# Softmax maxima in a fused attention and gated-MLP kernel: GpSimd keeps the maximum over partitions, VectorE takes the rest

## The chip, the cores and the metric

The kernel runs on one core of a Trainium2 chip. The metric is the device time of one execution in microseconds, as the median of several runs. A core has TensorE (PE, matrix products), VectorE (DVE), ScalarE (ACT), GpSimd (POOL) and SyncE (SP), which here only starts transfers. Each works through its own instructions in order. The work of an instruction starts when the semaphores it waits for have been raised, and whatever stands behind a waiting instruction on the same engine waits with it.

## The reference

```python
g = sigmoid((x * gate_w).sum(-1, keepdims=True))     # x: [1, 2048, 448]
q, k, v = split_heads(x @ wqkv)                      # 16 heads of 28
scores = einsum("bhqd,bhkd->bhqk", q, k) * 28 ** -0.5
a = (softmax(scores) @ v) @ wo
gate = x @ W_gate                                    # 448 -> 1792
h = (gate * (gate > 0)) * (x @ W_up)
b = h @ W_down                                       # 1792 -> 448
out = g * a + (1 - g) * b
```

Everything is float32. The products of the projections and of the MLP are made from a high and a low part of each operand, eleven matmuls ("passes") for one product of 448 terms.

## The kernel before

There are three stretches. The first projects q, k and v and writes q and k to DRAM. The second is the attention, with part of the MLP's gate and up products mixed in. The third holds what is left of these, the output projection and the down projection.

The attention is done in 32 rounds. Round v does one visit: head v // 2 and one half of its 16 key tiles of 128, against all 2048 queries in 4 blocks of 512 (`TB`). A visit has 16 score pairs. One pair is two matmuls into one score buffer of two PSUM banks (`score`, L250 to L267); there are three such buffers, taken in turn by `ps_w`, and the row maxima use the same three.

For 12 of the 16 pairs (query blocks 0 to 2) the maximum of each query over all keys is known ahead. It comes from "row maxima" (`smax`, L161 to L176): the scores are made a second time with queries on partitions, two matmuls into a score buffer, and VectorE reduces them (L171). The maxima of a head are turned round and written into extra rows of Q (`smax_end`), so that the matmul subtracts them itself, and ScalarE applies exp straight from PSUM (L262). Each round has 12 row maxima except the last three, which have none.

The other 4 pairs (query block 3) take another way:

- ScalarE copies the pair from PSUM into a P tile in SBUF (L264).
- `block_max` (L211 to L232) takes a running maximum over the key tiles on VectorE, elementwise into the tile `rm` (L224, L225, L227, L230). In a head's second visit it starts from the maximum of the first.
- `all_max` (L236) has GpSimd take the maximum over the 128 partitions.
- `take_max` (L241) subtracts it from the P tile, four key tiles at once (128 x 2048); two of these make the four pairs.
- `take_exp` (L248) has ScalarE apply exp in place.

`pv` (L593 to L611) then multiplies P by V, in two parts of 32 matmuls each; the second visit's result is added to the first's. `rescale` (L574 to L589) scales the first visit's result for query block 3 by exp of the difference of the two maxima: a subtraction (L585), an exp (L588), a product (L589), once in every second round.

The MLP's units are passes (`gu_mm`, L547) followed by a ReLU on ScalarE (L557) and a product on VectorE (L560); the result h is sent to DRAM (`spill_h`, L566). Weights are split on ScalarE and GpSimd in the first rounds (`split_f`) and reloaded by SP later (`load_f`, L539).

The order of everything in a round is written out by hand, one mark per step, as strings: FIRST for round 0, LONG for most, WIDE for four rounds with 44 passes instead of 33, LATE for the last three. The marks:

```text
s  a score pair (with its copy or exp)     m  a row maximum
x  one pass of the MLP                     n  a head's row maxima turned round
A  all_max                                 d, g  take_max on VectorE, on GpSimd
e  take_exp                                c, f  rescale, first and second step
w  split the weights of the next round     P, Q  the two parts of PV
```

`AHEAD` says how many of the next visit's pairs are already scored at the end of a round; these are always pairs of query block 3.

Of the kernel before, what the change touches and what calls it, by code (L numbers as in the profile page):

```python
# [13 lines left out]
OP = mybir.AluOpType  # L14
# [5 lines left out]
P = 128  # L20
# [9 lines left out]
TB = 512  # L30
NK = S // P
# [6 lines left out]

EARLY = (5, 4, 4, 3, 2, 2, 1, 1)

AHEAD = 2

NP = 10

FIRST = "xxxmxAsmxlsumxxxsmxxsmxsmxsmsmxsgxmdsexxxmexxmsxxmwxPQ"

LONG = "mmnsxxxsxxxsxxssmxxsxxsxxAmsxxxsmsxxgmxsxmxsxsxcmsxexxmxgmsxfxsexxxmmPwQ"

WIDE = "msxsxxsxxxsxmnxAxxxsmxxxxssxxxmxxxsxxssxxmxsxxmmxsxgexxmxxgmxxxCsxxsxmxxsmxeFsxmwPQ"

LATE = "ssnxxsxxxxxxsxsxxxxxssxxxxxxxsxssxxAdxxsxxxxdsxsxexCxsxxxsxxexfxwsxxxPQ"

ROUNDS = [(FIRST, 2)] + [(WIDE, 4) if k % 7 == 2 else (LONG, 3) for k in range(2 * H - 4)] + [(LATE, 4)] * 3

# [12 lines left out]
def gated_mix_kernel(ctx, tc, x, wq, wo, wgu, wd, out):  # L67
    nc = tc.nc
# [23 lines left out]
    def ps_w(name):  # L92
        if turns[0] is not None:
            turns[0] += 1
            if turns[0] % 3 == 0:
                return third[0].tile([P, 2, TB], F32, tag="w", bufs=1, name=name)
        return psum.tile([P, 2, TB], F32, tag="mx", bufs=2, name=name)

    def ps_x(name):
        return psum.tile([P, TB], F32, tag="x", bufs=2, name=name)  # L100
# [23 lines left out]
    h_d = {}  # L124
# [8 lines left out]
    def last_q(name, dt=F32R):  # L133
        return vp.tile([P, 4, TB], dt, name=name, tag="Q2", bufs=1)

    def p_slot(k, name, dt=F32):
        if k in (5, 6):
            return V[:, k - 3].rearrange("p k h d -> p (k h d)").rearrange("p (j t) -> p j t", t=TB)
        return (vp if k < 5 else att).tile([P, 4, TB], dt, name=name, tag=f"P{k}", bufs=1)
# [50 lines left out]
    AT, QUAD, slots = {}, {}, iter(range(10 ** 6))  # L190
# [17 lines left out]
    todo_max, todo_sub, todo_exp, todo_all = [], [], [], []  # L208
    RM = {}

    def block_max(v, j, k, q):  # L211

        n = TQ[v // 2]
        b = j - NB + n
        if (v, b) not in RM:
            if b == 0:
                rm = att.tile([P, max(TQ), TB], F32, name=f"rm_{v}", tag=f"rm{v % 2}", bufs=1)
                for c in range(n):
                    RM[v, c] = rm[:, c]
        r, p = RM[v, b], QUAD[q]  # L220
        c = k % 4
        if k % (NK // 2) == 0:
            if v % 2:
                nc.vector.tensor_tensor(r, p[:, c], RM[v - 1, b], op=OP.max)  # L224
                nc.vector.tensor_tensor(r, p[:, c + 1], r, op=OP.max)  # L225
            else:
                nc.vector.tensor_tensor(r, p[:, c], p[:, c + 1], op=OP.max)  # L227
        else:
            for d in range(2):
                nc.vector.tensor_tensor(r, p[:, c + d], r, op=OP.max)  # L230
        if k % (NK // 2) == NK // 2 - 2:
            todo_all.append((v, b, [(v, j, i) for i in (k // 4 - 1, k // 4)]))  # L232

# [2 lines left out]
        nc.gpsimd.partition_all_reduce(RM[v, b], RM[v, b], P, bass_isa.ReduceOp.max)  # L236
        todo_sub.extend((v, b, q) for q in quads)

    def take_max(engine):
        v, b, q = todo_sub.pop(0)  # L240
        engine.tensor_tensor(QUAD[q], QUAD[q], RM[v, b].unsqueeze(1).to_broadcast([P, 4, TB]), op=OP.subtract)  # L241
        todo_exp.append(q)

    def take_exp():
# [5 lines left out]
    def score(late=True):  # L250

        v, done, q, half, chunks = stream.pop(0)
        h = v // 2
        if q not in QUAD:
            QUAD[q] = p_slot(next(slots) % NP, f"P_{v}_{q[1]}_{q[2]}")
        ps = ps_w(f"s_{v}_{chunks[0][0]}_{chunks[0][1]}")
        for c, (k, j) in enumerate(chunks):
            nc.tensor.matmul(ps[:, c], K[h % 3][:, k * P:(k + 1) * P], Q[h][:, j * TB:(j + 1) * TB], start=True, stop=True)  # L258
            AT[v, k, j] = QUAD[q][:, 2 * half + c]
        dst = QUAD[q][:, 2 * half:2 * half + 2]  # L260
        if done:
            nc.scalar.activation(dst, ps, AF.Exp, scale=SCALE)  # L262
        else:
            nc.scalar.activation(dst, ps, AF.Copy)  # L264
            todo_max.append((v, chunks[0][1], chunks[0][0], q))
        while late and todo_max:
            block_max(*todo_max.pop(0))  # L267

    X = {}

# [17 lines left out]
    with tc.tile_pool(name="qkv", bufs=1) as pa:  # L288
# [135 lines left out]
        ps = ps_x("warm_ps")  # L424
# [130 lines left out]
    def relu(i, ps):  # L555
        RL[i] = fe.tile([P, TB], F32, name=f"rl_{i}", tag="rl", bufs=2)
        nc.scalar.activation(RL[i], ps, AF.Relu)  # L557

    def hidden(i, ps, h):
        nc.vector.tensor_tensor(h, ps, RL.pop(i), op=OP.mult)  # L560

    def spill_h(i, ps):
        h = fe.tile([P, TB], F32, name=f"h_{i}", tag="h", bufs=2)
        hidden(i, ps, h)
        h_d[i] = dram.tile([P, TB], F32, name=f"h_d_{i}")
        nc.gpsimd.dma_start(h_d[i], h)  # L566


    NI = H * NK
    OS, LS = {}, {}  # L570

    RS = {}

    def rescale(v, part, engine):  # L574

        h = v // 2
        n = TQ[h]
        if v % 2 == 0 or n == 0:
            return
        rows = slice(32 * (NB - n), P)  # L580
        if part == 0:
            RS[h] = fe.tile([P, TB], F32, name=f"rs_{h}", tag="rb", bufs=1)
            for b in range(n):
                r = slice(32 * (NB - n + b), 32 * (NB - n + b) + 32)
                engine.tensor_tensor(RS[h][r], RM[v - 1, b][r], RM[v, b][r], op=OP.subtract)  # L585
        else:
            d = RS.pop(h)[rows]
            nc.scalar.activation(d, d, AF.Exp, scale=SCALE)  # L588
            engine.tensor_tensor(OS[h][rows], OS[h][rows], d, op=OP.mult)  # L589

    PO = {}

# [69 lines left out]
    for v, (order, nu) in enumerate(ROUNDS):  # L662
        todo = list(range(nxt, nxt + nu))
        nxt += nu
        small_things(2 * v)
        passes = [(*divmod(k, 2), n) for k in todo for n in range(NT)]
        units = []
        ns = 0
        for o in order:
            if o == "x" and not passes:  # L670
                continue
            if o == "s":
                ns += 1
                if ns == 8:
                    small_things(2 * v + 1)
                if stream:
                    score()
            elif o == "m":
                if m < len(maxima):
                    smax(m)  # L680
                    m += 1
            elif o == "x":
                i, half, n = passes.pop(0)
                if n == 0:
                    units.append((i, half, ps_x(f"gu_{i}_{half}")))
                gu_mm(units[-1][2], i, half, n)
                if n == NT - 1:
                    i, half, ps = units.pop()
                    spill_h(i, ps) if half else relu(i, ps)
                    if half:  # L690
                        load_f(i + 2)
            elif o == "n":
                if v % 2 and v < 2 * H - 1:
                    smax_end(v // 2 + 1)
            elif o == "w":
                ready = nxt + (ROUNDS[v + 1][1] if v + 1 < len(ROUNDS) else 2)
                ready = min(ready + ready % 2, 2 * NF)
                while parts < ready:
                    split_f(parts // 2, act_high, pool_low, (parts % 2,))
                    parts += 1  # L700
                    if parts % 2 == 0:
                        fetch_f(parts // 2 + 1)
            elif o == "A":
                all_max()
            elif o == "d":
                take_max(nc.vector)
            elif o == "g":
                take_max(nc.gpsimd)
            elif o == "e":
                take_exp()  # L710
            elif o in "cCfF":
                rescale(v, "cf".index(o.lower()), nc.gpsimd if o in "cf" else nc.vector)
            elif o == "l":
                sends.pop()()
            elif o == "u":
                split_f(0, act_high, pool_low, (1,))
                QS.append(last_q("Q2"))
                nc.gpsimd.memset(f32(QS[2])[96:128], 0.0)
                load_k(2)
                load_q(2)  # L720
                fetch_f(2)
                parts = 2
            elif o in "PQ":
                pv(v, "PQ".index(o))
        left = [k for k in todo_exp + todo_sub + todo_all if k[0] == v]
        assert not passes and not left and v not in PO or len(stream) == max(0, 16 * (2 * H - 1 - v) - AHEAD), (v, passes, left, len(stream) + 16 * (v + 1))
    assert not stream and m == len(maxima), (len(stream), m)
# [183 lines left out]
```

## Time and profile before

| | us |
|---|---|
| median of 3 runs | 1543.4 (1539.19 to 1546.63) |
| the profiled execution | 1536.65 |
| its span, first to last instruction | 1534.9 |

| engine | busy us | share of the span |
|---|---|---|
| TensorE, matmul | 1296.2 | 84% |
| VectorE | 899.7 | 59% |
| ScalarE | 772.5 | 50% |
| GpSimd | 523.1 | 34% |

The mean clock granted to TensorE is 0.926 of full speed. Rounds end with the copy or addition of the PV result: round 0 at 181.42 us of the span, round 28 at 1234.55, round 31 at 1326.91. "Busy" of TensorE is modelled and contains the overlap of matmuls in its pipeline, so that 84% doesn't mean that only 16% can be won.

In the rows of the profile, `a <- b` names what an instruction writes and reads, `xN` is a count, and a bracket at the end of a timeline row tells how long the engine stood idle before it and what released it.

### The profile page before, as it was taken

The page shows a single profiled execution, that of the slowest core. Times are in us where ns is not written, and L with a number is a line of the kernel's source. Part 1 is how long each engine was busy: PE and PEld are TensorE (multiplying, and loading weights), DVE is VectorE, ACT ScalarE, POOL GpSimd, SP SyncE. Part 2 cuts the span into 40 slices and gives each one's busy share as a digit, 9 for nine tenths or more (in the row PEclk, how much of TensorE's full clock was granted, in tenths as well). Part 3 has the DMA queues.
Part 4 walks back from the last instruction along what each step waited for, and adds up shares of the span by engine and source line. Part 5 has one row for each costly group of instructions (what it writes and reads, how often), then busy time and mean ns, then how long its engine had stood idle before and what let it go on. Part 6 is the DMA issues. An engine that isn't in the chain of part 4 may idle for free. (4 is left out here: it accounts for less than half of the span.)

```text
span 1534.9 us, 17075 instructions
## 1 busy us (share of the span) xinstructions
PE 1296.2 (84%) x6431; PEld 880.0 (57%) x6431; DVE 899.7 (59%) x939; ACT 772.5 (50%) x894; POOL 523.1 (34%) x327
## 2 busy tenths in 40 slices
PE   9997897887877789797978978778879788999998
PEld 6885554554544456464645545445545444689998
DVE  6465675565656557575755756666657533355333
ACT  5224675665555456475645655555646555522221
POOL 4221444435352333333333342524334211253110
PEclk9999898998989899898989989899999889999999
DMA  9663642333324232231425232313251122573442
GB/s 315 227 244 123 189 96 102 107 95 97 100 79 136 96 106 74 82 98 58 137 71 140 75 89 90 94 62 94 69 164 47 63 68 82 182 229 115 134 141 80
DMA packets 60687, 178.38 MB, mean 116 GB/s; under 512 B 13730, under 2 KB 20578, under 8 KB 55970
## 3 DMA queue, kind: packets, MB, share of 16 engines
q1 hardware_dynamic: 49388, 136.32, 30.5%
q0 software_dynamic: 10784, 40.51, 7.0%
q8 instruction: 51, 0.84, 0.2%
q10 hardware_dynamic: 432, 0.46, 0.1%
q14 instruction: 32, 0.26, 0.1%
HBM read 118.58 MB, written 58.87 MB: 116 GB/s over the span
## 5 line engine op out<-in xcount | busy, mean ns | idle before, releaser
L171 DVE TENSOR_REDUCE mx<-sm 128x1 f32<-128x1024 f32 x384 | 461.7, 1221 | 177.2 <-PE sm L169 176.9
L169 PE MATMUL sm<-K,Q 128*128 128x512 f32 x768 | 254.3, 419 | 172.9 <-ACT P L264 122.0
L547 PE MATMUL gu<-X,wg 128*128 128x512 f32 x1232 | 381.3, 400 | 17.4 <-POOL wg L112 11.6
L258 PE MATMUL s<-Q,K 128*128 128x512 f32 x1024 | 321.1, 401 | 25.2 <-ACT P L262 21.5
L262 ACT ACTIVATE P<-s 128x1024 f32<-128x1024 f32 x306 | 299.3, 1026 | 44.6 <-PE s L258 40.2
L169 PEld LDWEIGHTS sm<-K,Q 128*128 128x128 f32 x768 | 139.9, 196 | 244.1 <-ACT P L264 129.9
L601 PE MATMUL po<-P,V 128*32 128x512 f32 x1640 | 265.6, 671 | 15.8 <-ACT rl L557 13.4
L547 PEld LDWEIGHTS gu<-X,wg 128*128 128x128 f32 x1232 | 233.7, 190 | 76.1 <-POOL wg L112 12.0
L241 POOL TENSOR_TENSOR P<-P,rm 128x2048 f32<-128x2048 f32 x45 | 204.0, 4537 | 159.9 <-issue 144.6
L258 PEld LDWEIGHTS s<-Q,K 128*128 128x128 f32 x1024 | 184.6, 190 | 87.6 <-ACT P L262 28.9
L248 ACT ACTIVATE P<-P 128x2048 f32<-128x2048 f32 x52 | 99.4, 1911 | 203.0 <-POOL P L241 182.0
L601 PEld LDWEIGHTS po<-P,V 128*32 128x32 f32 x1640 | 66.8, 122 | 165.3 <-issue 141.9
L264 ACT ACTIVATE P<-s 128x1024 f32<-128x1024 f32 x104 | 104.5, 1019 | 75.3 <-PE s L258 73.0
L566 POOL DMA_DIRECT2D h_d<-h x56 | 38.3, 683 | 304.7 <-DVE h L560 288.5
L810 PE MATMUL acc<-WD,hh 128*128 128x448 f32 x672 | 138.5, 365 | 0.0
L601 PE MATMUL po<-V 128*32 128x512 f32 x408 | 136.1, 673 | 0.6 <-ACT V L248 0.6
L236 POOL PARTITION_ALL_REDUCE rm<-rm x32 | 57.6, 1801 | 230.1 <-DVE rm L230 81.7
L810 PEld LDWEIGHTS acc<-WD,hh 128*128 128x128 f32 x672 | 126.2, 188 | 10.4
L230 DVE TENSOR_TENSOR rm<-P,rm 128x512 f32<-128x512 f32 x156 | 118.1, 757 | 22.2 <-ACT P L264 14.8
L103 ACT ACTIVATE hh<-hr 128x512 fp32r<-128x512 f32 x56 | 35.3, 632 | 119.0 <-PE acc L810 116.5
L262 ACT ACTIVATE V<-s 128x1024 f32<-128x1024 f32 x78 | 77.2, 1026 | 24.7 <-PE s L258 24.0
L227 DVE TENSOR_TENSOR rm<-P 128x512 f32<-128x512 f32 x13 | 37.5, 2888 | 88.0 <-ACT P L264 87.1
(86 smaller groups left out, 1026.6 us busy)
## 6 DMA issues: line engine op xcount, KB each, us to landing
wg<-ws_d SPq DMA_DIRECT2D x42, 896.0 KB
K<-qk_d SPq DMA_DIRECT2D x64, 224.0 KB
Q<-qk_d SPq DMA_DIRECT2D x64, 224.0 KB
h_d<-h POOLq DMA_DIRECT2D x56, 256.0 KB, 2.5
hr<-h_d SPq DMA_DIRECT2D x56, 256.0 KB
ws_d<-wg SPq DMA_DIRECT2D x14, 896.0 KB
qk_d<-st POOLq DMA_DIRECT2D x21, 512.0 KB, 3.2
wgr<-wgu SPq DMA_DIRECT2D x13, 512.0 KB
```

The lines of the kernel that those rows point to most:

```text
L169: nc.tensor.matmul(ps[:, c, :], Q[h][:, u * P:(u + 1) * P], K[h % 3][:, k0:k0 + TB], start=True, stop=True)
L171: nc.vector.tensor_reduce(MX[h][:, 2 * u + half:2 * u + half + 1], ps, axis=AX.XY, op=OP.max)
L230: nc.vector.tensor_tensor(r, p[:, c + d], r, op=OP.max)
L236: nc.gpsimd.partition_all_reduce(RM[v, b], RM[v, b], P, bass_isa.ReduceOp.max)
L241: engine.tensor_tensor(QUAD[q], QUAD[q], RM[v, b].unsqueeze(1).to_broadcast([P, 4, TB]), op=OP.subtract)
L248: nc.scalar.activation(q, q, AF.Exp, scale=SCALE)
L258: nc.tensor.matmul(ps[:, c], K[h % 3][:, k * P:(k + 1) * P], Q[h][:, j * TB:(j + 1) * TB], start=True, stop=True)
L262: nc.scalar.activation(dst, ps, AF.Exp, scale=SCALE)
L264: nc.scalar.activation(dst, ps, AF.Copy)
L547: nc.tensor.matmul(ps, WS[i][:, s, a], xf(i // NF, b), start=(n == 0), stop=(n == NT - 1))
L601: nc.tensor.matmul(po[32 * j:32 * j + 32], V[:, h // 4 % 2, k, h % 4], AT.pop((v, k, j)), start=(k == k0), stop=(k == k0 + NK // 2 - 1))
L810: nc.tensor.matmul(ACC[i // NF][t][:, :D], HH[i][:, a, t * P:(t + 1) * P], WD[:, f, b], start=(f == 0 and n == 0), stop=(f == NF - 1 and n ...
```

## The change

- `block_max` reads the scores from PSUM instead of from ScalarE's copy in SBUF (only the pairs scored before round 0 still use the copy). The first maximum of a head takes one tile from PSUM and the other from the copy, as VectorE takes one operand from PSUM here.
- `take_max` is always on VectorE; before, 57 of its 64 instructions were GpSimd's (`g`).
- `rescale`'s subtraction and product are always on VectorE; before, they were GpSimd's in LONG and partly in LATE.
- The transfer of h to DRAM is started by SP instead of GpSimd.
- Three pairs of the next visit are scored ahead instead of two.
- All four order strings are new. In LONG, A moves from the 26th mark to the 5th, and the two `take_max` to the 35th and 60th.

```diff
-AHEAD = 2
+AHEAD = 3
-FIRST = "xxxmxAsmxlsumxxxsmxxsmxsmxsmsmxsgxmdsexxxmexxmsxxmwxPQ"
-LONG = "mmnsxxxsxxxsxxssmxxsxxsxxAmsxxxsmsxxgmxsxmxsxsxcmsxexxmxgmsxfxsexxxmmPwQ"
-WIDE = "msxsxxsxxxsxmnxAxxxsmxxxxssxxxmxxxsxxssxxmxsxxmmxsxgexxmxxgmxxxCsxxsxmxxsmxeFsxmwPQ"
-LATE = "ssnxxsxxxxxxsxsxxxxxssxxxxxxxsxssxxAdxxsxxxxdsxsxexCxsxxxsxxexfxwsxxxPQ"
+FIRST = "AmxmxsmxmxxlxsxumsmmmxxxsxdxxxsxssmxxmxsmmxdexxsxsewsPQ"
+LONG = "ssmnAxxxxsmxsxmxsmxxxmsmxxxsmxxmxsdxsxxxsxsmxxxsmxxmexxsmxxdxxcsxsefwsPQ"
+WIDE = "smnmxxxxxxxsxxmxxxxmsxmxxsmxxsAmxsxmxxsxsmxdxsxxsssxxxmxxxcsxmsxxdxxmxxxxexsxewsPfQ"
+LATE = "snwsxxAxdxxxsxxsxxxsxxdsxxxxcsxxsxxxsxxxsxxxxsxsxxxxsxxxxxexxxsxxessPfQ"
...
-        r, p = RM[v, b], QUAD[q]
-        c = k % 4
-        if k % (NK // 2) == 0:
-            if v % 2:
-                nc.vector.tensor_tensor(r, p[:, c], RM[v - 1, b], op=OP.max)
-                nc.vector.tensor_tensor(r, p[:, c + 1], r, op=OP.max)
-            else:
-                nc.vector.tensor_tensor(r, p[:, c], p[:, c + 1], op=OP.max)
+        r = RM[v, b]
+        if k % (NK // 2):
+            parts = [(p[:, c], r) for c in range(2)]
+        elif v % 2:
+            parts = [(p[:, 0], RM[v - 1, b]), (p[:, 1], r)]
         else:
-            for d in range(2):
-                nc.vector.tensor_tensor(r, p[:, c + d], r, op=OP.max)
+            parts = [(p[:, 0], q[:, 1])]
+        for x, y in parts:
+            nc.vector.tensor_tensor(r, x, y, op=OP.max)
...
-    def take_max(engine):
+    def take_max():
         v, b, q = todo_sub.pop(0)
-        engine.tensor_tensor(QUAD[q], QUAD[q], RM[v, b].unsqueeze(1).to_broadcast([P, 4, TB]), op=OP.subtract)
+        nc.vector.tensor_tensor(QUAD[q], QUAD[q], RM[v, b].unsqueeze(1).to_broadcast([P, 4, TB]), op=OP.subtract)
...
             nc.scalar.activation(dst, ps, AF.Copy)
-            todo_max.append((v, chunks[0][1], chunks[0][0], q))
-        while late and todo_max:
-            block_max(*todo_max.pop(0))
+            job = (v, chunks[0][1], chunks[0][0], ps if late else dst, dst)
+            if late:
+                block_max(*job)
+            else:
+                todo_max.append(job)
...
-        nc.gpsimd.dma_start(h_d[i], h)
+        nc.sync.dma_start(h_d[i], h)
...
-                engine.tensor_tensor(RS[h][r], RM[v - 1, b][r], RM[v, b][r], op=OP.subtract)
+                nc.vector.tensor_tensor(RS[h][r], RM[v - 1, b][r], RM[v, b][r], op=OP.subtract)
...
-            engine.tensor_tensor(OS[h][rows], OS[h][rows], d, op=OP.mult)
+            nc.vector.tensor_tensor(OS[h][rows], OS[h][rows], d, op=OP.mult)
```

More of the change, by code (lines that the diff above doesn't have):

```diff
@@ L209, in gated_mix_kernel, with block_max @@
     RM = {}
-    def block_max(v, j, k, q):
+    def block_max(v, j, k, p, q):
         n = TQ[v // 2]
@@ L572, in gated_mix_kernel, with rescale @@
     RS = {}
-    def rescale(v, part, engine):
+    def rescale(v, part):
         h = v // 2
@@ L705, in gated_mix_kernel @@
             elif o == "d":
-                take_max(nc.vector)
-            elif o == "g":
-                take_max(nc.gpsimd)
+                take_max()
             elif o == "e":
                 take_exp()
-            elif o in "cCfF":
-                rescale(v, "cf".index(o.lower()), nc.gpsimd if o in "cf" else nc.vector)
+            elif o in "cf":
+                rescale(v, "cf".index(o))
             elif o == "l":
```

## The prediction, made before the changed kernel was run

> **What bounds the kernel now.** I read the page first, then the waits, then the timeline of one pair of rounds.
>
> ```profile
> span 1534.9 us, 17075 instructions
> PE 1296.2 (84%) x6431; PEld 880.0 (57%) x6431; DVE 899.7 (59%) x939; ACT 772.5 (50%) x894; POOL 523.1 (34%) x327
> ...
> ACT P L248 <- POOL P L241: 182.0, 37, 11.5
> ...
> PE sm L169 <- ACT P L264: 122.0, 18, 11.0
> ...
> PE sm L169 <- ACT V L264: 41.5, 6, 11.1
> ...
> PE s L258 <- ACT P L262: 21.5, 4, 7.3
> ...
> PE po L601 <- ACT rl L557: 13.4, 3, 6.9
> ...
> PE gu L547 <- POOL wg L112: 11.6, 1, 11.6
> ```
>
> No engine is full, TensorE (PE) is the busiest, and it idles in few, long waits: 122.0 + 41.5 us in 24 waits for the ScalarE copy on L264. ScalarE itself waits 182.0 us for GpSimd's subtraction (L241). The timeline of one round shows the chain:
>
> ```profile
> 684.54 0.59 POOL L566 DMA_DIRECT2D h_d<-h  x1 [11.94 <-DVE h L560]
> 691.36 1.80 POOL L236 PARTITION_ALL_REDUCE rm<-rm  x1 [6.23 <-ACT rl L557]
> 700.25 8.98 POOL L241 TENSOR_TENSOR P<-P,rm 128x2048 f32<-128x2048 f32 x2 [7.09 <-issue]
> 704.77 1.91 ACT L248 ACTIVATE P<-P 128x2048 f32<-128x2048 f32 x1 [11.12 <-POOL P L241]
> 706.59 1.92 ACT L264 ACTIVATE P<-s 128x1024 f32<-128x1024 f32 x2
> 707.64 1.22 PE L169 MATMUL sm<-K,Q 128*128 128x512 f32 x2 [10.63 <-ACT P L264]
> ...
> L241 POOLq MODIFY_POOL_CONFIG  x56: 37/98/98, 189.4 to 1209.6; - x56
> ```
>
> GpSimd works in order. Its h_d transfer waits for VectorE until 684.5. About 6 us pass before the maximum over partitions and 7.09 us between it and the first subtraction, in which the profile names no other work: GpSimd's sequencer has a MODIFY_POOL_CONFIG ahead of each (the last row shows 56 of them on L241), called its switch below. The subtraction takes 4.5 us, ScalarE's exp waits 11.12 us for it, the copies of the next pairs queue behind that exp, their score buffers in PSUM stay full, and TensorE stands still for 10.63 us. The pair of matmuls after it takes 1.22 us, against 0.63 below: the clock has dropped to half.
>
> What is a round without its long wait?
>
> ```profile
> 181.42 0.60 ACT L607 ACTIVATE os<-po 128x512 f32<-128x512 f32 x1 [6.52 <-PE po L601]
> ...
> 676.62 0.69 DVE L609 TENSOR_TENSOR os<-po,os 128x512 f32<-128x512 f32 x1 [0.48 <-issue]
> 717.01 0.60 ACT L607 ACTIVATE os<-po 128x512 f32<-128x512 f32 x1 [5.84 <-PE po L601]
> 739.70 0.73 PE L169 MATMUL sm<-K,Q 128*128 128x512 f32 x2 [2.21 <-ACT P L264]
> 749.17 0.69 DVE L609 TENSOR_TENSOR os<-po,os 128x512 f32<-128x512 f32 x1 [0.49 <-issue]
> ...
> 1234.55 0.60 ACT L607 ACTIVATE os<-po 128x512 f32<-128x512 f32 x1 [7.11 <-PE po L601]
> 1259.37 1.06 PE L601 MATMUL po<-P,V 128*32 128x512 f32 x2 [6.88 <-ACT rl L557]
> 1292.72 6.28 PE L601 MATMUL po<-P,V 128*32 128x512 f32 x32 [6.15 <-ACT rl L557]
> 1326.91 0.69 DVE L609 TENSOR_TENSOR os<-po,os 128x512 f32<-128x512 f32 x1 [6.10 <-issue]
> ```
>
> Each round ends with one of the rows of L607 or L609. The 28 LONG and WIDE rounds take 1234.55 − 181.42 = 1053.1 us. Two LONG neighbours take 40.4 and 32.2 us; without their long waits (10.63, 2.21) they take 29.8 and 29.9. In the first of these some 1 us is slow clock (an estimate from the 1.22), so I take **29.3** for a LONG round whose wait is gone, and 28.6 as its lower end.
>
> **The change: VectorE's load.**
>
> ```profile
> 181.40:1229.00 1047.60, 849.68 (x4298) 525.50 (x4302) 666.45 (x661) 597.88 (x637) 399.27 (x197) 0.91 0.33 95
> ...
> L171 DVE TENSOR_REDUCE mx<-sm 128x1 f32<-128x1024 f32 x384 | 461.7, 1221 | 177.2 <-PE sm L169 176.9
> L230 DVE TENSOR_TENSOR rm<-P,rm 128x512 f32<-128x512 f32 x156 | 118.1, 757 | 22.2 <-ACT P L264 14.8
> L264 ACT ACTIVATE P<-s 128x1024 f32<-128x1024 f32 x104 | 104.5, 1019 | 75.3 <-PE s L258 73.0
> L560 DVE TENSOR_TENSOR h<-gu,rl 128x512 f32<-128x512 f32 x56 | 38.4, 686 | 36.9 <-ACT rl L557 23.2 <-PE gu L547 4.9 <-ACT V L262 4.4
> L227 DVE TENSOR_TENSOR rm<-P 128x512 f32<-128x512 f32 x13 | 37.5, 2888 | 88.0 <-ACT P L264 87.1
> L224 DVE TENSOR_TENSOR rm<-P,rm 128x512 f32<-128x512 f32 x13 | 25.5, 1960 | 88.2 <-ACT P L264 88.2
> L241 DVE TENSOR_TENSOR P<-P,rm 128x2048 f32<-128x2048 f32 x7 | 15.8, 2288 | 22.2 <-POOL rm L236 22.2
> L585 DVE TENSOR_TENSOR rs<-rm,rm 32x512 f32<-32x512 f32 x4 | 2.8, 688 | 0.1
> ...
> 659.63 4.61 POOL L241 TENSOR_TENSOR P<-P,rm 128x2048 f32<-128x2048 f32 x1 [7.12 <-issue]
> 659.93 0.68 DVE L560 TENSOR_TENSOR h<-gu,rl 128x512 f32<-128x512 f32 x1
> ...
> 666.36 4.56 POOL L241 TENSOR_TENSOR V<-V,rm 128x2048 f32<-128x2048 f32 x1
> 667.19 4.27 DVE L227 TENSOR_TENSOR rm<-P 128x512 f32<-128x512 f32 x1 [2.34 <-ACT P L264]
> ```
>
> The window holds 27.9 rounds (1047.6 / 37.6), so VectorE (DVE) works 666.45 / 27.9 = 23.9 us in each. Added: two subtractions of 2.29 us (L241 on DVE) = 4.6, and the rescaling's two steps in every second round, 0.69 each (L585) = 0.7. Removed: the slow maxima. The first maximum of a visit takes 2.89 or 1.96 us instead of 0.69, because GpSimd's subtraction runs beside it (667.19 beside 666.36): 1.7 us a round, and 7 hundredths on each of some six others (0.757), 0.4. An instruction of VectorE with one input in PSUM takes 0.68 in the same neighbourhood (659.93 beside 659.63), so I price a maximum from PSUM at 0.69, from 0.68 to at worst the 2.89 of L227. New sum: 23.9 + 4.6 + 0.7 − 2.1 = **27.1 us** a round. It fits under 29.3, with 2.2 to spare. ScalarE keeps its 597.88 / 27.9 = 21.4.
>
> [...]
>
> **The chain.** The maximum over partitions (A) now stands five marks into a LONG round, the first subtraction (d) 30 marks later, the second late. The switch and the all-reduce, 6.2 + 1.8 us, lie under the scores between A and d: 6 score pairs, 7 row maxima and 16 passes.
>
> ```profile
> 712.91 4.03 PE L601 MATMUL po<-P,V 128*32 128x512 f32 x33
> ...
> 719.17 0.63 PE L258 MATMUL s<-Q,K 128*128 128x512 f32 x2
> ...
> 719.63 0.86 PE L547 MATMUL gu<-X,wg 128*128 128x512 f32 x3
> ```
>
> Three matmuls take 0.86, two 0.63: a step of 0.23. So A to d is (26 + 16) × 0.23 = 9.7 us, and the row maxima there hold VectorE for 7 × 1.22 = 8.5. In WIDE it is 18 steps, 4.1 us, which covers the all-reduce; the switch has the 31 marks ahead of A. In LATE d is right behind A, but no row maximum queues behind it. In the first ten rounds the splits of weights still force a switch; in the later ones the built program gives GpSimd only all-reduces and small fills, and no switch. The long waits (the table's 163.5, and 21.5 in WIDE) therefore go.
>
> What is late next is a score buffer. There are three, in turn. A pair whose maxima are taken is now held for ScalarE's copy (1.02) and then two maxima (1.38): the built program makes VectorE wait for the copy. Of the four such pairs three stand ahead of P and Q, whose 64 matmuls take 7 us (33 in 4.03); VectorE's 4.1 us for them, and 2.1 of rescaling and addition in odd rounds, hide there, as do two copies, an exp and a third copy of ScalarE (5.0 us; 1.91 for the exp on L248). If that cover is missing, TensorE waits for the difference. The fourth pair is the first after Q: 0.63 + 1.02 + 1.38 = 3.0 us, and 0.6 before it for the copy of po (L607). The next user of its buffer stands s, s, m and four passes later, 10 steps = 2.3 us. So TensorE waits 3.6 − 2.3 = **1.3 us** in each LONG round, which I take for WIDE too, from 0 to 3 if VectorE lags.
>
> [...]
>
> At nothing go: h_d on SP instead of GpSimd. SP then waits for VectorE's L560 with the next load of weights (wg) queued behind it, and every K and Q load behind that; the buffer is first used 22 passes later, over half a LONG round, which hides a few us; uncovered, it costs TensorE what the load is late. Three pairs ahead: the copies need slots of P whose readers were the PV of a round ago. The first round keeps its 11.6 us (L547 for wg on L112): GpSimd's order there is the same. The feed-forward end is untouched.
>
> **Sum.** LONG: 29.3 + 1.3 = 30.6. WIDE has eleven more passes: 29.3 + 2.5 + 1.3 = 33.1. 24 × 30.6 + 4 × 33.1 = 866.8 for the 1053.1, so 186.3 less. The three LATE rounds (92.4 us) lose their two waits for ScalarE (6.88 + 6.15), 13.0, as A stands early there too. The profiled execution took 1536.65 us, 1.75 more than its span; 1536.65 − 199.3 = 1337.3. The median is 6.75 above that execution: **1344 us**.
>
> **Rivals.**
> 1. VectorE becomes the bound. For: 27.1 of 29.3, in order, with waits for TensorE and ScalarE at each end of a round. Against: it had whole waits of 10 us to lose until now. If it idles 6.7 us of a round, LONG takes 33.8, 28 × 3.2 = 90 more: 1434.
> 2. A is still late, and d, at the head of VectorE, waits for it with the row maxima queued behind. For: the weight splits in the first ten rounds stand right ahead of A in GpSimd's queue. A full switch of 7.09 in each: 1344 + 71 = 1415. Against: 9.7 us of cover, and a switch waits for nothing once the splits are done.
> 3. Slower: a maximum from PSUM is slow. 7.5 maxima a round; at 2.89 us each VectorE needs 27.1 + 7.5 × 2.2 = 43.6 us a round, 28 × 6.0 = 168 over the present 37.6: 1711. It decides from 0.69 + (37.6 − 27.1) / 7.5 = 2.1 us for one. Against it stands 659.93.
> 4. The change doesn't remove the wait but moves it: ScalarE's second exp waits for VectorE's second d, and Q for that exp, as long as it now does (6 us a round on the mean). About 1543. For: d and exp are the last before P. Against: 2.29 replaces 4.5, and P's 3.5 us lie between.
>
> **How the numbers follow.** Forecast 0.62, rival 1 0.20, rival 2 0.06, rival 3 and like troubles 0.08, rival 4 0.04. Low end: 28.6 a round and no new wait give 24 × 28.6 + 4 × 31.1 = 810.8, hence 1288; I cut at 1300. High end: rival 1, 1435. Of rival 4 0.03 lies within 0.5% (about what a measurement of this kernel can tell) and 0.01 above. Faster 0.88, same 0.03, slower 0.09.
>
> **What would show it.** Right: waits of 10 us of TensorE for the copy are gone, round ends 30 to 31 us apart, maxima at 0.69, 64 subtractions on VectorE at 2.29, VectorE near 27 us a round, small waits at the third pair of a round. Wrong: round ends over 33 apart with VectorE busy throughout (1), idle VectorE ahead of its subtraction (2), maxima over 1 us (3), PV waiting for the exp (4).

## The result, and the profile after

| | us |
|---|---|
| before, median of 4 runs | 1541.6 (1539.19 to 1546.63) |
| after, median of 4 runs | 1285.1 (1281.88 to 1291.3) |
| ratio | 0.8337, 95% interval 0.8299 to 0.8376 |

The change takes a sixth off the time. The direction and the cause were forecast (1344 us), but the time lies below the range (1300 to 1435). The first two rows below are from the page of the changed kernel. The others are waits over the whole span: who waited, for whom, then the microseconds in all, how many waits, and the longest one. A line number is that of the run's own kernel, so that L256 here is L258 of the kernel before.

```profile
span 1280.1 us, 16867 instructions
PE 1241.6 (97%) x6431; PEld 872.5 (68%) x6431; DVE 962.1 (75%) x1022; ACT 776.1 (61%) x894; POOL 191.2 (15%) x188
...
POOL rm L234 <- DVE rm L228: 618.8, 23, 29.4
...
DVE rm L228 <- ACT P L262: 64.8, 37, 8.1
...
PE s L256 <- DVE rm L228: 11.2, 17, 0.8
```

TensorE is busy for 97%. Its waits for the copy have gone from the list. Now GpSimd waits for VectorE, 618.8 us in all: in 23 of the 32 cases it is idle when the running maximum arrives. The largest of TensorE's new waits come to 11.2 us, in 17 waits for the maxima from PSUM, none longer than 0.8. TensorE is also busy for 54.6 us less (1296.2 before, 1241.6 now) with the same 6431 matmuls, and its granted clock is 0.994 instead of 0.926: a part of the gain is that it no longer works at half the clock behind long waits (run 12 looks at this: behind a wait of 9.86 us four matmuls take 2.07 us there, 1.09 in the changed kernel).

The groups of the moved work (times and sizes, then busy us and mean ns of one, then the engine's idle time before them and what ended it):

```profile
L228 DVE TENSOR_TENSOR rm<-s,rm 128x512 f32<-128x512 f32 x218 | 150.4, 690 | 74.6 <-ACT P L262 57.3 <-ACT V L262 10.0 <-DVE rm L228 0.5
L234 POOL PARTITION_ALL_REDUCE rm<-rm x32 | 57.2, 1788 | 673.7 <-DVE rm L228 618.8 <-DVE mx L171 30.0 <-PE s L256 12.0
...
L239 DVE TENSOR_TENSOR P<-P,rm 128x2048 f32<-128x2048 f32 x52 | 117.9, 2272 | 5.8 <-POOL rm L234 5.8
L246 ACT ACTIVATE P<-P 128x2048 f32<-128x2048 f32 x52 | 99.4, 1914 | 5.3 <-DVE P L239 4.5
```

A maximum from PSUM takes 0.690 us, a subtraction 2.27. ScalarE's exp on these tiles waited 182.0 us for GpSimd; now it waits 4.5 us for VectorE. The ends of rounds 0, 14, 15, 28 and 31, from the timeline:

```profile
177.60 0.60 ACT L607 ACTIVATE os<-po 128x512 f32<-128x512 f32 x1 [0.54 <-PE po L601]
...
588.92 0.60 ACT L607 ACTIVATE os<-po 128x512 f32<-128x512 f32 x1 [3.04 <-PE po L601]
617.84 0.69 DVE L609 TENSOR_TENSOR os<-po,os 128x512 f32<-128x512 f32 x1 [0.82 <-PE po L601]
...
999.27 0.60 ACT L607 ACTIVATE os<-po 128x512 f32<-128x512 f32 x1 [3.04 <-PE po L601]
...
1073.73 0.69 DVE L609 TENSOR_TENSOR os<-po,os 128x512 f32<-128x512 f32 x1 [3.98 <-PE po L601]
```

Rounds 1 to 28 take 999.27 − 177.60 = 821.67 us instead of 1053.13, so 231.5 less; the LATE rounds 74.5 instead of 92.4, 17.9 less; round 0 ends 3.8 us sooner, and the end after round 31 is 1.6 us shorter. That is the whole 254.8 us. A LONG round takes 28.9 us (617.84 − 588.92).

The start of round 15, from the timeline, shows the new wait whole:

```profile
588.79 1.20 PE L256 MATMUL s<-Q,K 128*128 128x512 f32 x4
588.92 0.60 ACT L607 ACTIVATE os<-po 128x512 f32<-128x512 f32 x1 [3.04 <-PE po L601]
589.55 1.02 ACT L262 ACTIVATE P<-s 128x1024 f32<-128x1024 f32 x1
...
590.61 1.42 DVE L228 TENSOR_TENSOR rm<-s,rm 128x512 f32<-128x512 f32 x2 [2.27 <-ACT P L262]
...
592.17 0.70 PE L256 MATMUL s<-Q,K 128*128 128x512 f32 x2 [0.69 <-DVE rm L228]
592.20 1.78 POOL L234 PARTITION_ALL_REDUCE rm<-rm  x1 [27.08 <-DVE rm L228]
```

The first pair is copied at 589.55, its maxima follow at 590.61 (VectorE had been idle for 2.27 us), and the third pair, which takes the same buffer, starts 0.69 us late. The maximum over partitions follows at once, without the 6 us that stood ahead of it before. In rounds 1 to 8, behind a weight split on GpSimd, 5.9 to 6.8 us still pass ahead of it:

```profile
243.87 1.80 POOL L234 PARTITION_ALL_REDUCE rm<-rm  x1 [5.89 <-DVE mx L171]
```

### The profile page after: what moved, and what is told of

Its sections match the earlier page's. It is cut to its first block, busy times and chain, and to the rows that moved or that the text cites. A ratio compares the mean times of both kernels' runs of the same rounds, so it can differ in the third digit from the quotient of the medians.

```text
span 1280.1 us, 16867 instructions
## 1 busy us (share of the span) xinstructions
PE 1241.6 (97%) x6431; PEld 872.5 (68%) x6431; DVE 962.1 (75%) x1022; ACT 776.1 (61%) x894; POOL 191.2 (15%) x188
## 4 chain that ended last, share of the span: by engine, by line
PE 89%; DVE 4%; ACT 2%; DMA 2%; issue 1%; POOL 1%; SPq 0%; POOLq 0%; ACTq 0%
PE gu L547 19%; PE s L256 19%; PE po L601 18%; PE sm L169 13%; PE acc L808 10%; PE qk L381 5%; DVE rm L228 3%; PE wo L767 3%; PE v L399 3%; ACT P L262 1%; DVE mx L171 1%; DMA wg<-ws_d 1%; DMA or<-o_d 0%; DMA wr<-wq 0%; ACT P L260 0%
## 5 line engine op out<-in xcount | busy, mean ns | idle before, releaser
L171 DVE TENSOR_REDUCE mx<-sm 128x1 f32<-128x1024 f32 x384 | 456.5, 1219 | 60.6 <-PE sm L169 59.5
L547 PE MATMUL gu<-X,wg 128*128 128x512 f32 x1232 | 373.9, 398 | 10.8 <-POOL wg L112 7.2
L260 ACT ACTIVATE P<-s 128x1024 f32<-128x1024 f32 x306 | 306.7, 1025 | 116.8 <-PE s L256 113.1
L256 PE MATMUL s<-Q,K 128*128 128x512 f32 x1024 | 319.5, 403 | 13.6 <-DVE rm L228 11.2
L256 PEld LDWEIGHTS s<-Q,K 128*128 128x128 f32 x1024 | 184.7, 189 | 99.3 <-DVE rm L228 10.9
L169 PE MATMUL sm<-K,Q 128*128 128x512 f32 x768 | 243.2, 398 | 7.5 <-DVE mx L171 3.6
L601 PE MATMUL po<-P,V 128*32 128x512 f32 x1640 | 227.3, 594 | 0.0
L228 DVE TENSOR_TENSOR rm<-s,rm 128x512 f32<-128x512 f32 x218 | 150.4, 690 | 74.6 <-ACT P L262 57.3
L169 PEld LDWEIGHTS sm<-K,Q 128*128 128x128 f32 x768 | 137.1, 188 | 52.6 <-ACT P L260 10.1
L234 POOL PARTITION_ALL_REDUCE rm<-rm x32 | 57.2, 1788 | 673.7 <-DVE rm L228 618.8
L262 ACT ACTIVATE P<-s 128x1024 f32<-128x1024 f32 x104 | 105.1, 1024 | 46.6 <-PE s L256 45.4
L239 DVE TENSOR_TENSOR P<-P,rm 128x2048 f32<-128x2048 f32 x52 | 117.9, 2272 | 5.8 <-POOL rm L234 5.8
L601 PE MATMUL po<-V 128*32 128x512 f32 x408 | 115.0, 594 | 0.0
L109 DVE TENSOR_TENSOR hh<-hr,hh 128x512 fp32r<-128x512 f32 x56 | 49.4, 883 | 62.2 <-ACT hh L103 62.2
L381 PE MATMUL qk<-X,W 128*128 128x512 f32 x308 | 77.4, 398 | 0.3 <-DVE X L109 0.2
```

Of the source, the lines that this page charges most:

```text
L169: nc.tensor.matmul(ps[:, c, :], Q[h][:, u * P:(u + 1) * P], K[h % 3][:, k0:k0 + TB], start=True, stop=True)
L171: nc.vector.tensor_reduce(MX[h][:, 2 * u + half:2 * u + half + 1], ps, axis=AX.XY, op=OP.max)
L228: nc.vector.tensor_tensor(r, x, y, op=OP.max)
L239: nc.vector.tensor_tensor(QUAD[q], QUAD[q], RM[v, b].unsqueeze(1).to_broadcast([P, 4, TB]), op=OP.subtract)
L381: nc.tensor.matmul(ps, W[:, a, c * P:(c + 1) * P], xf(tb, b), start=(n == 0), stop=(n == NT - 1))
L547: nc.tensor.matmul(ps, WS[i][:, s, a], xf(i // NF, b), start=(n == 0), stop=(n == NT - 1))
```

## The experiments

Three theories were set against each other first. "Slow subtraction": GpSimd's subtraction and the switch ahead of it (the 6 to 7 us without named work between two kinds of work on GpSimd) were the wait. "GpSimd": all the gain is in emptying its queue. "Late maximum", or "orders": what counts is how far the steps of the chain stand apart. A time is the median of four runs, and a ratio is to the kernel before, measured beside it, with a 95% interval.

**1. Subtraction alone on VectorE**

```diff
             elif o == "g":
-                take_max(nc.gpsimd)
+                take_max(nc.vector)
```

> The kernel before with one edit: the 57 subtractions that GpSimd did are VectorE's; old orders, maxima from the copy, rescaling and the transfer of h still on GpSimd. Theory 'slow subtraction' (GpSimd's 4.5 us and the 7.1 us switch ahead of it are the wait): the exp starts 9 us sooner in the slow rounds, LONG near 29 us, 1330 us or below. Theory 'late maximum' (what counts is when the maximum over partitions can start; GpSimd's queue of h and the switch stay ahead of it): the wait passes to VectorE, which holds the row maxima behind the subtraction; round pairs still uneven, 1400 to 1450 us.

1466.5 us, ratio 0.952 (0.950 to 0.955). Its waits:

```profile
POOL h_d L566 <- DVE h L560: 570.7, 50, 22.5
...
POOL rm L236 <- DVE rm L230: 110.3, 12, 11.6
...
POOL rs L585 <- issue: 87.9, 12, 8.8
...
POOL rm L236 <- issue: 75.5, 12, 6.9
```

Less than a third of the gain. GpSimd's queue still has the transfers of h, and 75.5 and 87.9 us pass ahead of the all-reduce and of the rescaling with no other work named. This is near what "late maximum" expected (1400 to 1450) and slightly above it.

**2. GpSimd with the maximum only, old orders**

```diff
+ (run 1), and in addition
-                rescale(v, "cf".index(o.lower()), nc.gpsimd if o in "cf" else nc.vector)
+                rescale(v, "cf".index(o.lower()), nc.vector)
-        nc.gpsimd.dma_start(h_d[i], h)
+        nc.sync.dma_start(h_d[i], h)
```

> The kernel before with the subtraction and the rescaling on VectorE and h sent by SP, so that GpSimd has only the maximum over partitions in most rounds; old orders, two pairs ahead, maxima from the copy. Theory 'GpSimd' (freeing it is the whole gain): 1280 to 1310 us. Theory 'orders' (the placement alone is not enough, the old places of the maximum and of the subtraction leave 3.4 us between them): 1350 to 1420 us.

1382.8 us, 0.898 (0.896 to 0.901): the placement is worth 156 us, and not all. The time lies where "orders" put it.

**3. All but the orders: run 2 with maxima from PSUM**

```diff
-AHEAD = 3
+AHEAD = 2
(FIRST, LONG, WIDE, LATE as before, with d for g, c for C, f for F)
```

> The changed kernel with the four old orders and two pairs ahead, so the run before this one plus maxima from PSUM. If holding the score buffer for copy and maxima in turn costs time, this is 10 to 40 us above that run; if reading PSUM helps VectorE (no slow maxima beside GpSimd), it is 0 to 15 us below it.

1447.9 us, 0.940 (0.938 to 0.942), 65 us above run 2, where 10 to 40 were expected of a buffer held longer. TensorE's waits of run 2, then of this run:

```profile
PE sm L169 <- DVE mx L171: 35.8, 21, 3.0
PE s L258 <- DVE mx L171: 31.8, 23, 1.6
```

```profile
PE sm L169 <- DVE mx L171: 52.9, 28, 2.4
PE s L256 <- DVE mx L171: 31.6, 22, 1.6
PE s L256 <- DVE rm L228: 22.1, 36, 2.9
...
PE sm L169 <- DVE rm L228: 7.6, 13, 1.3
```

In the old orders the maxima from PSUM add 46.6 us to TensorE's waits for score buffers that VectorE still holds. Without new orders this part of the change loses.

**4. The orders alone**

```diff
(the changed kernel, with)
+        engine = nc.gpsimd if v < 2 * H - 3 else nc.vector   # take_max
-            job = (v, chunks[0][1], chunks[0][0], ps if late else dst, dst)
+            job = (v, chunks[0][1], chunks[0][0], dst, dst)
(h_d and both steps of rescale on nc.gpsimd)
```

> The changed kernel's orders and three pairs ahead, with all else as before: subtraction (but for the last three rounds), rescaling and h on GpSimd, maxima from the copy. Theory 'late maximum': the maximum now starts a round early and 16 us lie between it and the first exp, against 6.2 + 1.8 + 7.1 + 4.5 = 19.6 us of GpSimd: waits of 3 to 5 us remain, 1360 to 1420 us. Theory 'slow subtraction' or 'GpSimd': 1480 us or more.

1446.1 us, 0.940 (0.936 to 0.943). The orders alone are worth some 93 us: more than "GpSimd" allows, and less than "late maximum" expected. The largest wait left of TensorE is that of its score pairs (`s`) for ScalarE's exp, 85.2 us in 22 waits of up to 6.4 us. VectorE has one that no theory named:

```profile
DVE rm L228 <- POOL rs L586: 95.5, 14, 9.8
```

VectorE's running maximum waits for the rescaling's subtraction, which queues on GpSimd behind both subtractions and reads the `rm` that is to be overwritten. Runs 5, 6 and 7 below each give back one part of the placement, for 7, 35 and 25 us; this run gives back all, for 161. No run gives back the rescaling alone, so its price, and how much the parts cost only together, stay open.

**5. Maxima from the copy**

```diff
-            job = (v, chunks[0][1], chunks[0][0], ps if late else dst, dst)
+            job = (v, chunks[0][1], chunks[0][0], dst, dst)
```

> The changed kernel with block maxima taken from ScalarE's copy in SBUF instead of PSUM, all else as changed. Theory 'held buffer' (the 0.7 to 0.8 us that TensorE waits at the third pair of a LONG round is the buffer held for the copy and then two maxima): that wait goes, 24 x 0.75 = 18 us less, 1262 to 1275 us. Rival 'PSUM frees VectorE' (maxima from SBUF are slow beside GpSimd): 1290 us or more.

1292.2 us, 0.838 (0.836 to 0.840): 7 us above the changed kernel. Rounds 9 and 28 end at the first two rows; the next two are the third and the fourth score pair of round 14, and the last row is a wait over the whole span:

```profile
451.55 0.69 DVE L609 TENSOR_TENSOR os<-po,os 128x512 f32<-128x512 f32 x1 [0.55 <-PE po L601]
...
1008.66 0.60 ACT L607 ACTIVATE os<-po 128x512 f32<-128x512 f32 x1 [3.04 <-PE po L601]
...
571.13 0.63 PE L256 MATMUL s<-Q,K 128*128 128x512 f32 x2
...
573.13 0.73 PE L256 MATMUL s<-Q,K 128*128 128x512 f32 x2 [0.68 <-DVE mx L171]
...
PE s L256 <- DVE mx L171: 16.1, 21, 2.5
```

In the changed kernel round 9 ends at 441.43 and round 28 at 999.27. All of the loss lies in the first nine rounds, where GpSimd still splits weights beside the maxima: there the 69 maxima take 58.6 us of VectorE against 47.1 in the changed kernel, and behind them 143 take 98.8 against 98.7. From round 10 on the rounds are equal in sum, most LONG ones near 28.9 us. At the third pair the wait did go (571.13 has no idle time before it), so the buffer was held there as "held buffer" says. But it comes back at the fourth pair (573.13), whose releaser is the row maximum (L171), which queues on VectorE behind the same block maxima. "Held buffer" alone was wrong. With run 2 at 1382.8, the orders on top of the placement are worth 91 us, as many as without it (93): the two effects, placement as a whole and orders, add up.

**6. Subtraction on GpSimd, all else as changed**

```diff
+        engine = nc.gpsimd if v < 2 * H - 3 else nc.vector
-        nc.vector.tensor_tensor(QUAD[q], QUAD[q], ...
+        engine.tensor_tensor(QUAD[q], QUAD[q], ...
```

> The changed kernel with the subtractions back on GpSimd except in the last three rounds. Switch theory: each round again has two switches and 9 us of subtraction between the maximum and the second exp, 1.8 + 7.1 + 4.5 = 13.4 us to the first exp, which stands 14 to 16 us behind: small waits at most for the first, for the second some; 1290 to 1340 us. If the subtraction's engine is what gave the gain: 1450 us or more.

1320.1 us, 0.856 (0.854 to 0.859). Round 9 ends at 471.93 (30.5 us later than in the changed kernel), round 28 at 1034.17 (34.9 later). So where splits share GpSimd's queue the subtraction costs 3 us a round; in the 19 rounds behind them, 0.23. There the new orders leave enough room even for the slow one.

**7. h on GpSimd**

```diff
-        nc.sync.dma_start(h_d[i], h)
+        nc.gpsimd.dma_start(h_d[i], h)
```

> The changed kernel with the transfers of h started by GpSimd again. With the maximum over partitions at the start of a round and its subtraction 9.7 us later, a start of 0.7 us and its wait for VectorE are covered: within 6 us of the changed kernel. If GpSimd's queue is tight: 1310 us or more.

1309.9 us, 0.850 (0.848 to 0.852), 25 us above the changed kernel: the expected 6 us were missed. Two waits, and two rows of GpSimd's timeline:

```profile
PE gu L547 <- POOL wg L112: 18.8, 5, 6.9
PE acc L808 <- POOL WD L112: 10.1, 1, 10.1
...
392.33 0.54 POOL L566 DMA_DIRECT2D h_d<-h  x1 [12.99 <-DVE h L560]
399.98 5.59 POOL L112 TENSOR_TENSOR wg<-wgr,wg 128x384 fp32r<-128x384 f32 x6 [7.11 <-issue]
```

The maximum over partitions did have its cover, but the weight splits behind the transfer did not, in the first ten rounds and once in the feed-forward end. (In the changed kernel the first row is one wait of 7.2 us, and the second isn't there.) Rounds 1 to 9 take 21.7 us more than in the changed kernel, rounds 10 to 28 nothing. The transfer itself takes 0.54 to 0.74 us of GpSimd; more lies behind it: 7.11 us without named work pass between it and the split. So this split starts 2.8 us behind the end of round 7 (397.19). In the changed kernel it starts 4.0 us ahead of that end (380.30 and 384.33), when ScalarE's part of it is done.

**8. Half the maxima**

```diff
-            parts = [(p[:, c], r) for c in range(2)]
+            parts = [(p[:, 0], r)]
```

> The changed kernel with the second maximum of most pairs left out (of each two key tiles only one is looked at, but for a head's first pair and a second visit's first), to price the held buffer and VectorE's load: 6 maxima of 7.5 a round become 3 or so, 2 us of VectorE. Held buffer: the wait of 0.7 us at the third pair goes, LONG 28.2 us, 1262 to 1270 us. If VectorE's load bounds the round: 2 us a round less, 1225 to 1240 us. If neither: 1285 us.

1264.4 us, 0.820 (0.818 to 0.822). Rounds 14 and 15, from the windows of TensorE to GpSimd (busy us and instructions of each, then the granted clock, the share of the DMA engines and GB/s):

```profile
551.34:607.66 56.32, 56.32 (x308) 36.44 (x309) 47.75 (x47) 41.95 (x43) 3.61 (x3) 1.00 0.38 106
```

28.2 us a round, with TensorE at work all the time by its matmul rows: I take this for a LONG round without its waits. (Its weight loads still show some tenths of a microsecond of idle time, and rounds 4, 6 and 8 take 27.8 to 28.0 us.)

**9 to 11. Moving passes, and the first split**

```diff
-LONG = "ssmnAxxxxsmxsxmxsmxxxmsmxxxsmxxmxsdxsxxxsxsmxxxsmxxmexxsmxxdxxcsxsefwsPQ"
+LONG = "ssmnAxxxxxxxsmxsxmxsmxxxmsmxxxsmxxmxsdxsxsxsmxxsmxxmexxsmxxdxxcsxsefwsPQ"   # run 9, 11
-FIRST = "AmxmxsmxmxxlxsxumsmmmxxxsxdxxxsxssmxxmxsmmxdexxsxsewsPQ"
+FIRST = "mxmxsmxmxxlxuAsxmsmmmxxxsxdxxxsxssmxxmxsmmxdexxsxsewsPQ"   # run 10, 11
```

> The changed kernel with three passes of LONG moved up: seven instead of four stand ahead of the round's third score pair, taken from two places later in the round. If the 0.7 to 0.8 us at the third pair is VectorE being late at the start of a round only, three passes (0.69 us) cover it: LONG 28.3 us, 24 x 0.6 = 14 us less, 1268 to 1274 us. If VectorE is short over the whole round, the wait comes back at the row maxima: 1282 to 1288 us.

> The changed kernel with another FIRST: the second half of the first weight split goes ahead of the maximum over partitions on GpSimd. In the changed kernel TensorE waits 7.2 us in round 0 for that split, behind the maximum and a switch. If the switch is the wait, 5 to 8 us less, 1277 to 1281 us; if the maximum then comes too late for the subtraction behind it, within 3 us of 1285.

> The two runs before this one together: if each does what it should, 20 us below the changed kernel, 1262 to 1268 us; if neither, 1285 us.

1296.7 us (0.843, 0.841 to 0.845), 1287.0 (0.837, 0.835 to 0.839) and 1297.8 (0.844, 0.842 to 0.846). None helps: run 9 comes out above both of its ranges, run 10 within the 3 us of its second case, and run 11 at run 9's time.

```profile
PE sm L169 <- ACT P L260: 9.6, 20, 1.1
...
PE sm L169 <- ACT V L260: 3.6, 7, 1.1
...
PEld sm L169 <- ACT P L260: 30.6, 84, 1.5
```

In run 9 the wait at the third pair falls from 11.2 us to 0.2, and row maxima wait for ScalarE's exp instead (2.2 and 1.1 us in the changed kernel). The last row has the same wait by TensorE's weight loads, which are the first to be late: 30.6 us, 10.1 in the changed kernel. It seems that the passes that were moved had given ScalarE its time. In run 10 TensorE waits for VectorE's row maxima instead of the split (11.7 us in two waits, 3.6 in the changed kernel).

**12. A long wait put back**

```diff
             elif o == "e":
+                if order is LONG and len(todo_exp) + len(todo_sub) == 2:
+                    for _ in range(16):
+                        nc.scalar.activation(idle, idle, AF.Copy)
                 take_exp()
(idle: a tile of 128 x 512 in SBUF, set to zero ahead of round 0)
```

> The changed kernel with sixteen idle copies of 0.6 us on ScalarE ahead of the first exp of each LONG round, so that TensorE gets a wait of several us again; nothing else changed. It prices the half clock behind a long wait. If TensorE's clock drops behind a wait as in the kernel before, a LONG round takes 28.9 us plus its new wait plus 1.5 us of slow clock; if the 1.5 us which the kernel before had beyond 28.2 + 10.6 in such a round were other small waits, 28.9 plus the wait and no more.

1573.4 us, 1.022 (1.020 to 1.025). One round, 41.17 us long (652.92 to 694.09), from TensorE's timeline:

```profile
683.67 2.07 PE L256 MATMUL s<-Q,K 128*128 128x512 f32 x4 [9.86 <-ACT P L260]
...
687.38 1.04 PE L601 MATMUL po<-V 128*32 128x512 f32 x2
...
688.24 0.62 PE L601 MATMUL po<-V 128*32 128x512 f32 x2
```

Behind 9.86 us of wait the four matmuls take 2.07 us, 1.09 in the changed kernel, and the PV matmuls get back to speed at 688.24. A stretch of 4.6 us at half the clock loses 2.3 us. 28.2 + 9.86 + 2.3 = 40.4 of the 41.17; 28.9 and the wait alone would be 38.8. So the clock does drop behind a long wait. In the kernel before the same can be read in TensorE's weight loads:

```profile
707.64 0.50 PEld L169 LDWEIGHTS sm<-K,Q 128*128 128x128 f32 x2 [11.07 <-ACT P L264]
...
709.65 0.18 PEld L601 LDWEIGHTS po<-P,V 128*32 128x32 f32 x2 [0.66 <-issue]
...
710.50 0.18 PEld L601 LDWEIGHTS po<-P,V 128*32 128x32 f32 x2 [0.66 <-issue]
...
711.18 0.12 PEld L601 LDWEIGHTS po<-V 128*32 128x32 f32 x3 [0.48 <-issue]
711.61 0.12 PEld L601 LDWEIGHTS po<-V 128*32 128x32 f32 x3 [0.31 <-issue]
```

Loads come 0.85 us apart at 709.65 and 710.50, and 0.43 apart from 711.18 on: some 3.5 us at half speed (707.64 to 711.18), an estimated 1.75 lost. In run 12 the slow stretch is longer, 4.6 us.

**13 to 15. What sets the 0.7 us**

```diff
-AHEAD = 3                                                  # run 13
+AHEAD = 4
-LONG = "ssmnAxxxxsmxsxmxsmxxxmsmxxxsmxxmxsdxsxxxsxsmxxxsmxxmexxsmxxdxxcsxsefwsPQ"
+LONG = "ssmnAxxxxsmxsxmxsmxxxmsmxxxsmxxmxsdxsxxxsxsmxxxsmxxmecxxsmxxdxxsxsefwsPQ"
(FIRST with one more s ahead of w)
+        engine = nc.gpsimd if 9 < v < 2 * H - 3 and q[2] % 2 == 0 else nc.vector   # take_max, run 14
```

> The changed kernel with four pairs ahead instead of three, so that no pair of the copy and maxima kind is left for the start of a round; LONG differs only in the rescaling's first step (c), which moves in front of the thirteenth score pair, FIRST by one score pair more at its end. If the 0.7 us a LONG round is the chain at its start (pair, copy, two maxima, row maximum), it now lies under P and Q: LONG 28.2 us, 1265 to 1272 us. If VectorE's load over the round sets it, or VectorE can't do eight maxima under P and Q: 1282 to 1300 us.

> The changed kernel with the first of the two subtractions of rounds 10 to 28 on GpSimd, where 14 to 16 us lie between the maximum over partitions and the exp against 1.8 + 7.1 + 4.5 us. It takes 2.3 us of load from VectorE and leaves the start of the round alone. If load sets the 0.7 us: LONG 28.2 us from round 10 on, 1270 to 1275 us. If the chain at the start does: 1283 to 1290 us.

> The changed kernel itself, beside the two runs before it on the same chip: 1282 to 1291 us, LONG 28.9 us.

1315.2 us (0.855, 0.854 to 0.857), 1288.7 (0.838, 0.837 to 0.840) and 1285.9 (0.836, 0.835 to 0.838). Run 14, first its page, then its waits:

```profile
PE 1244.0 (97%) x6431; PEld 872.9 (68%) x6431; DVE 921.4 (72%) x1003; ACT 775.7 (60%) x894; POOL 279.3 (22%) x207
...
PE s L257 <- DVE rm L228: 11.2, 17, 0.8
```

VectorE has 41 us less to do than in run 15 (962.5), and the wait at the start of a round stays at 11.2 us in 17 times, as in run 15. So load does not set it. Run 8 took about as much load from VectorE, but with it the second maximum out of the chain at the start of the round, and there the wait went: the chain sets it. Run 13 puts that chain under P and Q, and VectorE can't do eight maxima there: TensorE's waits for its maxima from PSUM grow from 11.2 to 12.9 us with up to 3.1 us in one, those of the score pairs for row maxima from 1.4 to 9.8, and LONG rounds take mostly 29.1 and 30.2 in turn. The run is slower than either of its theories had it. No run beats the changed kernel with its work whole.

## Why the prediction was right or wrong

**What bounds the kernel: right.** The long waits for the copy (163.5 us) were GpSimd's chain, and they are gone. Run 12 puts such a wait back into each LONG round and loses all of the gain.

**The base of a round, 29.3 us: the step that failed.** Run 8 shows 28.2. I took 29.8 and 29.9 us from two rounds less one wait each, and allowed 1 us of slow clock in the first only. In the first, 1.75 us were slow clock, and the weight load waited 11.07 us where the matmul row shows 10.63: 40.39 − 11.07 − 1.75 = 27.6. In the second I missed a wait. TensorE's weight loads in that round have two:

```profile
739.70 0.30 PEld L169 LDWEIGHTS sm<-K,Q 128*128 128x128 f32 x2 [2.65 <-ACT P L264]
...
745.45 0.11 PEld L601 LDWEIGHTS po<-P,V 128*32 128x32 f32 x1 [1.51 <-ACT P L248]
```

Loads of this kind stand 0.3 us apart without any wait (711.61 above), so the second is 1.2 us late: 32.16 − 2.65 − 1.2 = 28.3. The matmul rows showed 2.21 and 0.60 for these, as the modelled end of a matmul eats into the wait behind it. The two results, 27.6 and 28.3, lie about the 28.2 that was measured. Rounds 1 to 28 take 803.9 us in run 8, where the bases of the forecast (29.3, and 31.8 for WIDE) come to 830.4: this step is worth 26.5 us. The range's low end stood on the same base (28.6) and was then cut from 1288 to 1300, so it could not hold the time.

**The new wait, 1.3 us: right in place and chain, too large.** It is 0.69 by its row, and 0.8 as round 15 differs from that of run 8 (28.92 and 28.11). I charged the copy of po in full ahead of the first pair's copy; it runs while the pair's matmuls do (588.92 to 589.52, the copy at 589.55), and the turn of the row maxima (n) stands in the cover too. All rounds 1 to 28 take 821.7 us, 17.7 more than in run 8, where 28 waits of 1.3 were to make 36.4: 18.7 us too many. Copy and maxima follow each other here (589.55, 590.61), as the program's waits make them, and no run shows them side by side.

**VectorE's sum, 27.1 us: near.** It is busy 26.4 and 25.4 us in rounds 14 and 15. A maximum from PSUM takes 0.690 us, the rescaling's subtraction from SBUF 0.689, and a subtraction on a P tile 2.27 us. Rivals 1 and 3 fall with it: VectorE's load is not the bound (run 14). Rival 4 falls on the 4.5 us that the exp waits for VectorE; rival 2 on a subtraction that waits 5.8 us in all for GpSimd.

**h to SP "at nothing": wrong, and hidden in the sum.** It is worth 25 us in the new orders (run 7), through the weight splits queued behind it. I had looked for what it delays on SP, and not for what it frees on GpSimd.

**The rest.** LATE lost 17.9 us against 13.0 forecast, the first round 3.8 against none. 45 + 5 + 4 + 2 us for rounds 1 to 28 (26.5 of base and 18.7 of wait), LATE, round 0 and the end make the 56 us by which the span fell further than the 199.3 of the forecast.

## What to carry to other kernels

To take a wait out of a steady loop, measure the loop's base where nothing waits: subtract all waits, those of the weight loads among them, and the slow-clock stretch behind each long one (3.5 to 4.6 us behind waits of 10 to 11 us here). A chain over four engines that work in order is shortened by where its steps stand as well as by who does them; here the two were worth 93 and 156 us and added up, and one part of the change (maxima from PSUM) lost 65 us in the old order and won 7 in the new. An engine with a costly switch between kinds of work (6 to 7 us on GpSimd here) is best given one kind, unless the order leaves room for the switch, as it did in the later rounds of run 6.

## What the runs showed of the hardware that I had not expected

A wait costs more than its length: behind 10 us, TensorE ran 3.5 to 4.6 us at half clock. Between an all-reduce and an elementwise instruction GpSimd lost 6 to 7 us each way (5.89 us ahead of an all-reduce behind a weight split, 7.09 ahead of a subtraction behind an all-reduce), more than the 4.5 us subtraction itself. A transfer started from GpSimd takes 0.54 to 0.74 us of it, and what is queued behind it waits with it, the 7.11 us ahead of a weight split too: 25 us in all in run 7.
